# Attention's 64 by 64 products in groups of four, sums of weights on GpSimd, and a test ahead of an addition

## The chip, the core and the metric

The kernel runs on one core of a Trainium2 chip. The metric is the device time of one execution in microseconds (us), lower is better; times given are medians of several runs. A core has a matrix engine (TensorE, PE in the profile, with its weight loads as PEld), a vector engine (VectorE, DVE), a scalar engine (ScalarE, ACT), GpSimd (POOL) and a sync engine (SP) that here only issues transfers. Matrix products land in PSUM, which has eight banks of 2 KB per partition.

## The reference, cut to what matters

```python
# q, k, v: (8, 8, 576, 64); w_in 512 x 2048, w_out 2048 x 512
scores = scale * np.matmul(q_c, k_c.transpose(0, 1, 2, 4, 3))   # chunks of 64 positions
scores = scores - np.max(scores, axis=-1, keepdims=True)
attn = np.exp(scores)
attn = attn / (np.sum(attn, axis=-1, keepdims=True) + 1e-09)
out = np.matmul(attn, v_c)
x = out.transpose(0, 2, 1, 3).reshape(4608, 512)
h = x @ w1_in;  r = np.maximum(h, 0.0);  y = (s * (r * r) + b) @ w1_out
h = y @ w2_in;  g = h / (1.0 + np.exp(-1.702 * h));  result = g @ w2_out
```

Attention works inside chunks of 64 positions, and two feed-forward layers follow. Weights arrive as 64-bit floats.

## The kernel before, in words

The 4608 tokens are nine blocks of 512. A block of attention is four pairs of heads, and a pair has eight chunks, so 16 products of 64 by 64 for the scores (L287) and 16 for the second product with v (L271). Head h of the pair lies in partitions 64h to 64h + 63, for q, k, v and the result alike, so the products alternate between two quarters of the array: rows and columns 0 to 63, and rows and columns 64 to 127. Scores and second products each take one PSUM bank, out of two that rotate (tag "at"). Blocks 0 and 1 use `EarlyPair`, which loads and transposes otherwise and whose second product (L358) already runs over all four quarters into two banks. `split` and `split_x` turn a result into a high and a low part: ACT copies (L96), DVE subtracts (L97).

Each large product is three matmuls of 128 x 512 (low by high, high by high, high by low); `gemm_in` (L487) and `gemm_out` (L562) are the first layer, and the first block of the second. The other eight blocks of the second layer go in pairs through `Halves`, with seven products in place of eight (L658, L753); for that `sums` prepares sums and differences of quarters of the second weights. It loads four quarters into a staging buffer, GpSimd computes four sums (L193 to L196), ACT copies the rounded high part into a second staging buffer (L198), GpSimd subtracts it (L199), and SP stores both (L204). There are three staging buffers, and 32 calls of `sums`.

`decode` turns 64-bit weights into 32-bit ones: ACT scales the low words into c (L120), DVE shifts and merges the high words into t, which is m by its bits (L121, L124), GpSimd adds c to t (L128), ACT squares the high words into c (L129), DVE sets m to zero where that square is tiny (L131). In the opening `first_steps` spreads this over steps and then splits m (L146, L147); for the second weights `decode_second` issues it at once and GpSimd stores m (L177).

The order of the work is a list of items with due times in units, 32 units to a block; items of one time stand in order of their entry. A pair whose offset is o issues its scores at o + 1, its softmax from o + 2, the second product at o + 8 and the split at o + 8.5. Offsets are 7 units apart, in block 2 8 units. In the opening the steps follow `FIRST_STEPS`. A planner that simulates the engines makes each engine's queue out of this; each queue then runs strictly in its order.

Of the kernel before, what the change touches and what calls it, by code (L numbers as in the profile page):

```python
# [44 lines left out]
def chunk_attention_two_ffn(ctx, tc, q, k, v, w1_in, w1_out, s, b, w2_in, w2_out, out):  # L45
# [32 lines left out]
    h_ps = ctx.enter_context(tc.tile_pool(name="h_ps", bufs=2, space=PSUM))  # L78
    at_ps = ctx.enter_context(tc.tile_pool(name="at_ps", bufs=2, space=PSUM))
    dpool = ctx.enter_context(tc.tile_pool(name="dpool", bufs=1, space=DRAM))  # L80
# [9 lines left out]
    wi_sums = [dpool.tile([P, 7, 2, 2, P], F32, name=f"wi_sums{i}") for i in range(KF // 2)]  # L90
    wo_sums = dpool.tile([P, 7, KF // 2, 2, 2, P], F32, name="wo_sums")
    y_dram = [dpool.tile([P, KD, n], F32, name=f"y{j}") for j, n in enumerate(sizes)]

# [22 lines left out]
    def decode(st, m, c):  # L116

        high, low = st[:, :, 1], st[:, :, 0]
        t = m.bitcast(I32)
        nc.scalar.activation(out=c.bitcast(I32), in_=low.bitcast(U32), func=AF.Copy, scale=2.0 ** -29)  # L120
        nc.vector.tensor_scalar(  # L121
            out=t, in0=high, scalar1=3, scalar2=0x3FFFFFF8, op0=ALU.logical_shift_left, op1=ALU.bitwise_and
        )
        nc.vector.scalar_tensor_tensor(  # L124
            out=t, in0=high, scalar=-0x40000000, in1=t, op0=ALU.bitwise_and, op1=ALU.bitwise_or
        )
        yield
# [56 lines left out]
    def sums(kind, i, z):  # L184
# [18 lines left out]
        for part, src in enumerate((hi.bitcast(F32), q[:, 1:8, :])):  # L203
            nc.sync.dma_start(out=to[:, :, part, :], in_=src)  # L204


    def runs(j):

        c0, n = starts[j] // CH, sizes[j] // CH
        done = 0  # L210
        while done < n:
            bb, c = divmod(c0 + done, CPB)
            step = min(n - done, CPB - c)
            yield done, step, bb, c
            done += step

    heads = [slice(h * CH, (h + 1) * CH) for h in range(2)]

    class Pair:
# [20 lines left out]
        def load_v(self):  # L240
            self.v = apool.tile([P, self.nch, CH], F32, tag="vs", name="vs", bufs=HP)
            for off, m, bb, c in runs(self.j):
                for h in range(2):
                    rows = v[bb, 2 * self.hp + h, c * CH:(c + m) * CH, :]
                    nc.sync.dma_start(
                        out=self.v[h * CH:(h + 1) * CH, off:off + m, :], in_=rows.rearrange("(c p) d -> p c d", p=CH)
                    )

# [7 lines left out]
        def turn(self, p):  # L256
# [8 lines left out]
            return pt  # L265

        def second(self, pt):
            ps = at_ps.tile([P, self.n], F32, tag="at", name="xT")
            for c in range(self.nch):
                for r in heads:  # L270
                    nc.tensor.matmul(  # L271
                        out=ps[r, c * CH:(c + 1) * CH], lhsT=self.v[r, c, :], rhs=pt[r, c, :], start=True, stop=True
                    )
            return ps

        def split_x(self, ps):
            X[0, self.j, self.hp] = xh, xl = new_x()
            split(xh, xl, ps)

        def steps(self):  # L280

            yield from self.stage_qk()
            yield
            ps = at_ps.tile([P, self.nch, CH], F32, tag="at", name="sc")
            for c in range(self.nch):
                for r in heads:
                    nc.tensor.matmul(  # L287
                        out=ps[r, c, :], lhsT=self.qt[r, c * CH:(c + 1) * CH], rhs=self.kt[r, c * CH:(c + 1) * CH],
                        start=True, stop=True,
                    )  # L290
# [4 lines left out]
            nc.vector.tensor_reduce(out=mx, in_=ps, axis=AX.X, op=ALU.max)  # L295
            nc.vector.tensor_tensor(
                out=p, in0=ps, in1=mx.unsqueeze(2).to_broadcast([P, self.nch, CH]), op=ALU.subtract
            )
# [11 lines left out]
            yield  # L310
            ps = self.second(turned)
            yield
            self.split_x(ps)
            done[0, self.j] = done.get((0, self.j), 0) + 1

    class EarlyPair(Pair):
# [21 lines left out]
        def turn(self, p):  # L338
# [7 lines left out]
            return pt.rearrange("p (c h q) -> p c h q", h=2, q=CH)  # L346

        def second(self, pt):

            n = self.n // 2  # L350
            banks = (
                at_ps.tile([P, n], F32, tag="at", name="xT"),
                acc_ps.tile([P, n], F32, tag=f"acc{2 * (self.hp % 2) + 1}", name="xT"),
            )
            for c in range(self.nch // 2):
                for e, ps in enumerate(banks):
                    for h, r in enumerate(heads):
                        nc.tensor.matmul(  # L358
                            out=ps[r, c * CH:(c + 1) * CH],
                            lhsT=self.early.v[c][heads[e], (2 * self.hp + h) * D:(2 * self.hp + h + 1) * D],  # L360
                            rhs=pt[heads[e], c, h, :], start=True, stop=True,
                        )
            return banks

        def split_x(self, banks):
            X[0, self.j, self.hp] = x = new_x()
            xh, xl = (t.rearrange("p (c e t) -> p c e t", e=2, t=CH) for t in x)
            for e, ps in enumerate(banks):
                split(xh[:, :, e, :], xl[:, :, e, :], ps.rearrange("p (c t) -> p c t", t=CH))
            if self.j == 0:  # L370
                first_x.update((i.engine, i) for i in nc.cur_bb.bb.instructions[-2:])
            elif self.hp == HP - 1:
                marks.update((("x", i.engine), i) for i in nc.cur_bb.bb.instructions[-2:])

# [38 lines left out]
    def new_x():  # L413
        return tuple(xpool.tile([P, NB_MAX], F32R, tag=t, name=t) for t in ("xh", "xl"))
# [164 lines left out]

    HF, HK = KF // 2, KD // 2  # L580

    def minus(to, one, two):
        nc.vector.tensor_tensor(out=to, in0=one, in1=two, op=ALU.subtract)

    class Halves:
# [58 lines left out]
        def bank(self, key, bank, *tags):  # L644
            pool, tag = {"x": (acc_ps, tags[0]), "d": (at_ps, "at"), "b": (h_ps, "h")}[bank]
            self.ps[key] = pool.tile([P, NB_MAX], F32, tag=tag, name=bank)
# [270 lines left out]
```

## Time and profile before

| | |
|---|---|
| median of 3 runs | 1655.07 us (1652.5 to 1656.92) |
| the profiled execution | 1660.28 us |
| its span | 1658.5 us |
| TensorE busy | 1604.2 us, 97% |
| VectorE, ScalarE, GpSimd busy | 69%, 45%, 16% |
| mean granted TensorE clock | 0.99 |

The profile is of one execution. Busy time is a union of intervals; a matmul's own duration in a row overlaps its neighbours, so the distance between starts is the pace. In a timeline row "x32" are 32 records merged, and a bracket gives the idle time ahead and who ended it. A product of 64 by 64 in 32-bit floats stands as two records.

### The profile page before, as it was taken

To read this page: it belongs to the slowest core of one execution; us is meant where nothing else is said; L and a number is where in the kernel's file an instruction comes from. 1 tells how busy PE (TensorE), PEld (TensorE's weight loads), DVE (VectorE), ACT (ScalarE), POOL (GpSimd) and SP (SyncE) were. 2 spreads that over 40 slices of the span, in tenths; PEclk is the share of its full clock that TensorE was granted. 3 is DMA by queue.
4 is the path that set the end of the run, shared out by engine and by line. 5 is a ranking of instruction groups with operands and counts; after the bars stand their busy time and mean duration, and the time that the engine had idled before them with its cause. 6 is when DMAs were issued, how large, how long until landed. Compare 5 with 4: busy or idle time off the path is not lost.

```text
span 1658.5 us, 24595 instructions
## 1 busy us (share of the span) xinstructions
PE 1604.2 (97%) x8928; PEld 1312.8 (79%) x8928; DVE 1149.3 (69%) x1836; ACT 747.0 (45%) x1258; POOL 266.9 (16%) x294
## 2 busy tenths in 40 slices
PE   6879999999999999999999999999999999999998
PEld 5758887778788878888888888878887888788876
DVE  5876666867687775777757543579568946984685
ACT  3768543333333333333345532456345525653552
POOL 1322101333223223233333000000001000100000
PEclk9889999999999999999999999999999999999999
DMA  9435445656455554646456441676868686767654
GB/s 229 114 102 162 121 132 131 146 132 163 122 141 145 143 136 132 156 128 155 117 160 216 135 135 45 188 239 221 206 195 266 181 221 207 255 183 218 219 192 77
DMA packets 398345, 272.19 MB, mean 164 GB/s; under 512 B 255376, under 2 KB 345488, under 8 KB 398224
## 3 DMA queue, kind: packets, MB, share of 16 engines
q1 hardware_dynamic: 390800, 249.64, 55.0%
q0 software_dynamic: 5120, 16.78, 3.0%
q10 hardware_dynamic: 2304, 4.20, 0.7%
q8 instruction: 71, 1.16, 0.3%
q14 instruction: 50, 0.41, 0.1%
HBM read 209.72 MB, written 60.82 MB: 163 GB/s over the span
## 4 chain that ended last, share of the span: by engine, by line
PE 77%; DVE 8%; DMA 4%; SPq 3%; ACT 3%; issue 2%; POOL 2%; POOLq 0%; DVEq 0%; ACTq 0%
PE acc L562 19%; PE h L487 18%; PE x L658 11%; PE x L753 11%; PE d L658 5%; PE d L753 5%; PE b L658 3%; PE b L753 3%; SPq L235 2%; PE sc L287 1%; PE xT L271 1%; DVE gl L502 1%; DVE r L500 1%; DVE pt L261 1%; ACT gh L501 1%
## 5 line engine op out<-in xcount | busy, mean ns | idle before, releaser
L487 PE MATMUL h<-xh,wi 128*128 128x512 f32 x1280 | 402.7, 396 | 13.5 <-ACT r L517 5.4
L562 PE MATMUL acc<-gh,wo 128*128 128x512 f32 x1152 | 354.8, 394 | 6.0 <-ACT gh L96 3.7
L487 PEld LDWEIGHTS h<-xh,wi 128*128 128x128 f32 x1280 | 240.3, 190 | 66.3 <-ACT r L517 6.3
L562 PEld LDWEIGHTS acc<-gh,wo 128*128 128x128 f32 x1152 | 215.5, 189 | 53.0 <-ACT gh L96 4.1
L487 PE MATMUL h<-xl,wi 128*128 128x512 f32 x640 | 251.2, 394 | 0.0
L562 PE MATMUL acc<-gl,wo 128*128 128x512 f32 x576 | 220.3, 392 | 3.8 <-DVE gl L502 3.8
L501 ACT ACTIVATE gh<-r,sb 128x512 fp32r<-128x512 f32 x112 | 80.9, 723 | 184.4 <-DVE r L500 184.1
L500 DVE SCALAR_TENSOR_TENSOR r<-r,sb 128x512 f32<-128x512 f32 x112 | 103.9, 928 | 64.3 <-ACT r L499 63.8
L502 DVE SCALAR_TENSOR_TENSOR gl<-r,sb,gh 128x512 fp32r<-128x512 f32 x112 | 107.3, 959 | 57.2 <-ACT gh L501 57.1
L487 PEld LDWEIGHTS h<-xl,wi 128*128 128x128 f32 x640 | 121.7, 190 | 25.9
L562 PEld LDWEIGHTS acc<-gl,wo 128*128 128x128 f32 x576 | 108.1, 188 | 28.6 <-DVE gl L502 6.2
L128 POOL TENSOR_TENSOR wm<-wm,wc 128x512 int32<-128x512 int32 x52 | 75.7, 1459 | 338.6 <-DVE wm L124 176.9
L730 ACT ACTIVATE op<-wo 128x512 fp32r<-128x512 f32 x128 | 79.5, 630 | 79.4 <-PE d L753 25.9
L680 DVE TENSOR_TENSOR wo<-wo,r 128x512 f32<-128x512 f32 x96 | 66.0, 691 | 63.0 <-ACT r L679 62.6
L753 PE MATMUL x<-op,wi 128*128 128x512 f32 x432 | 104.4, 389 | 0.0
L658 PE MATMUL x<-xh,wi 128*128 128x512 f32 x320 | 99.5, 391 | 3.1 <-DVE wo L677 3.1
L261 DVE STREAM_TRANSPOSE pt<-p 32x256 f32<-32x256 f32 x224 | 97.7, 436 | 3.9
L597 POOL DMA_DIRECT2D xr<-y x32 | 17.3, 540 | 506.3 <-DVE op L731 262.8
L679 ACT ACTIVATE r<-wo 128x512 f32<-128x512 f32 x96 | 60.8, 633 | 76.8 <-DVE wo L677 76.0
L753 PEld LDWEIGHTS x<-op,wi 128*128 128x128 f32 x432 | 81.1, 188 | 16.9
L731 DVE TENSOR_TENSOR op<-wo,op 128x512 fp32r<-128x512 f32 x128 | 85.2, 680 | 7.4 <-ACT op L730 6.0
L198 ACT ACTIVATE wst<-wst 128x896 fp32r<-128x896 f32 x32 | 30.5, 953 | 128.1 <-POOL wst L196 83.5
(145 smaller groups left out, 2780.1 us busy)
## 6 DMA issues: line engine op xcount, KB each, us to landing
wi<-wo_sums SPq DMA_DIRECT2D x112, 512.0 KB, 3.9
wi<-wi_sums SPq DMA_DIRECT2D x96, 512.0 KB, 3.7
wst<-in_moe_w_out SPq DMA_DIRECT2D x32, 512.0 KB, 4.6
wi_sums<-wst SPq DMA_DIRECT2D x32, 448.0 KB, 3.6
wo_sums<-wst SPq DMA_DIRECT2D x32, 448.0 KB, 3.5
wst<-in_moe_w_in SPq DMA_DIRECT2D x24, 512.0 KB, 5.0
y<-ost SPq DMA_DIRECT2D x36, 256.0 KB, 3.3
xr<-y POOLq DMA_DIRECT2D x32, 256.0 KB, 6.1
```

The lines of the kernel that those rows point to most:

```text
L128: nc.gpsimd.tensor_tensor(out=t, in0=t, in1=c.bitcast(I32), op=ALU.add)
L261: nc.vector.transpose(out=pt[r.start + ek * BK:r.start + (ek + 1) * BK, :, eq * BK:(eq + 1) * BK], in_=p[r.start + eq * BK:r.start + (eq + ...
L487: nc.tensor.matmul(out=ps, lhsT=w_[:, kk, :], rhs=x_, start=kk == 0 and a == 0, stop=kk == KD - 1 and a == 2,)
L500: nc.vector.scalar_tensor_tensor(out=r, in0=r, scalar=s_ap, in1=r, op0=ALU.mult, op1=ALU.mult)
L501: nc.scalar.activation(out=gh, in_=r, func=AF.Identity, bias=b_ap)
L502: nc.vector.scalar_tensor_tensor(out=gl, in0=r, scalar=b_ap, in1=gh.bitcast(F32), op0=ALU.add, op1=ALU.subtract)
L562: nc.tensor.matmul(out=acc[m], lhsT=l_, rhs=r_, start=i == 0 and a == 0, stop=i == KF - 1 and a == 2)
L658: nc.tensor.matmul(out=self.ps[key], lhsT=l_, rhs=r_, start=start and k == 0 and a == 0, stop=k == HK - 1 and a == 2, skip_group_check=not ...
L680: nc.vector.tensor_tensor(out=g, in0=h, in1=r, op=ALU.mult)
L730: nc.scalar.activation(out=hi, in_=src, func=AF.Copy)
L731: nc.vector.tensor_tensor(out=lo, in0=src, in1=hi.bitcast(F32), op=ALU.subtract)
L753: nc.tensor.matmul(out=self.ps[key], lhsT=l_, rhs=r_, start=start and i == 0 and a == 0, stop=i == HF - 1 and a == 2, skip_group_check=not ...
```

## The change

Four things are edited. (1) One PSUM tile of two banks, `at_banks`, stays for the whole kernel; scores go into the left halves of both banks and second products into the right halves. Chunks of the first half of a block write bank 0 and run as before; chunks of the second half write bank 1 and cross over: the scores of head h land in the partitions of the other head, v is loaded into crossed partitions, and the second product crosses back. `quarters` issues chunk i for both heads and chunk i + 4 for both heads, so that four products in a row have four different quarters of the array. `load_v` cuts its loads at the half of the block. `EarlyPair` of block 0 takes banks of tag "h" and "acc" for its second product. `Halves` alternates by hand between the two banks. (2) In `sums` the copy of the high part and both stores move to GpSimd. (3) In `decode` the square goes to the low words of the staged weights, and the test comes ahead of GpSimd's addition.

```diff
-    at_ps = ctx.enter_context(tc.tile_pool(name="at_ps", bufs=2, space=PSUM))
+    at_ps = ctx.enter_context(tc.tile_pool(name="at_ps", bufs=1, space=PSUM))
+    at_banks = at_ps.tile([P, 2, NB_MAX], F32, name="at")
...
         yield
+        square = low.bitcast(F32)
+        nc.scalar.activation(out=square, in_=high.bitcast(F32), func=AF.Square)
+        nc.vector.scalar_tensor_tensor(out=m, in0=square, scalar=TINY * TINY, in1=m, op0=ALU.is_ge, op1=ALU.mult)
+        yield
         nc.gpsimd.tensor_tensor(out=t, in0=t, in1=c.bitcast(I32), op=ALU.add)
-        nc.scalar.activation(out=c, in_=high.bitcast(F32), func=AF.Square)
-        yield
-        nc.vector.scalar_tensor_tensor(out=m, in0=c, scalar=TINY * TINY, in1=m, op0=ALU.is_ge, op1=ALU.mult)
         yield
...
-        nc.scalar.activation(out=hi, in_=q[:, 1:8, :], func=AF.Copy)
+        nc.gpsimd.tensor_copy(out=hi, in_=q[:, 1:8, :])
...
-            nc.sync.dma_start(out=to[:, :, part, :], in_=src)
+            nc.gpsimd.dma_start(out=to[:, :, part, :], in_=src)
...
+    left, right = at_banks[:, :, 0:NB_MAX // 2], at_banks[:, :, NB_MAX // 2:NB_MAX]
+
+    def quarters(nch):
+        for i in range(nch // 2):
+            for e in range(2):
+                for h in range(2):
+                    yield e, i, e * (nch // 2) + i, h, heads[h], heads[h ^ e]
...
+                for e in range(2):
+                    a, z = max(off, e * half), min(off + m, (e + 1) * half)
+                    for h in range(2) if a < z else ():
+                        rows = v[bb, 2 * self.hp + h, (c + a - off) * CH:(c + z - off) * CH, :]
+                        nc.sync.dma_start(
+                            out=self.v[heads[h ^ e], a:z, :], in_=rows.rearrange("(c p) d -> p c d", p=CH)
+                        )
...
         def second(self, pt):
+            for e, i, c, h, r, other in quarters(self.nch):
+                nc.tensor.matmul(
+                    out=right[r, e, i * CH:(i + 1) * CH], lhsT=self.v[other, c, :], rhs=pt[other, c, :],
+                    start=True, stop=True,
+                )
...
+            ps = self.room_scores().rearrange("p e (c t) -> p e c t", t=CH)
+            for e, i, c, h, r, other in quarters(self.nch):
+                nc.tensor.matmul(
+                    out=ps[other, e, i, :], lhsT=self.qt[r, c * CH:(c + 1) * CH], rhs=self.kt[r, c * CH:(c + 1) * CH],
+                    start=True, stop=True,
+                )
...
+        def room_scores(self):
+            return right if self.j == 0 and self.hp % 2 else left
...
+            if self.j == 0:
+                self.ps = (
+                    h_ps.tile([P, n], F32, tag="h", name="xT"),
+                    acc_ps.tile([P, n], F32, tag=f"acc{2 * (self.hp % 2) + 1}", name="xT"),
+                )
+            else:
+                self.ps = right[:, 0, :], right[:, 1, :]
...
         def bank(self, key, bank, *tags):
+            if bank == "d":
+                self.ps[key] = at_banks[:, next(turns) % 2, :]
+                return
```

## Rows read from the trace of the kernel before

**Rows 1.** The page, busy us with share of the span, and instructions.
```profile
PE 1604.2 (97%) x8928; PEld 1312.8 (79%) x8928; DVE 1149.3 (69%) x1836; ACT 747.0 (45%) x1258; POOL 266.9 (16%) x294
```

**Rows 2.** The chain that ended last, share of the span by engine.
```profile
PE 77%; DVE 8%; DMA 4%; SPq 3%; ACT 3%; issue 2%; POOL 2%; POOLq 0%; DVEq 0%; ACTq 0%
```

**Rows 3.** Stretches: length, busy PE, PEld, DVE, ACT, POOL, granted clock, DMA, GB/s.
```profile
46.00:125.00 79.00, 64.88 (x495) 51.38 (x494) 62.63 (x103) 55.23 (x103) 24.39 (x18) 0.89 0.33 103
...
235.00:310.00 75.00, 70.62 (x478) 55.72 (x474) 52.42 (x90) 29.39 (x48) 13.01 (x14) 1.00 0.56 136
310.00:440.00 130.00, 125.64 (x815) 102.74 (x814) 94.93 (x155) 43.80 (x70) 37.56 (x42) 0.99 0.58 143
440.00:570.00 130.00, 130.00 (x842) 107.01 (x841) 97.77 (x155) 47.24 (x76) 39.80 (x45) 1.00 0.53 133
```

**Rows 4.** Timeline of PE at two places: start, length, instructions merged.
```profile
83.26 0.69 PE L358 MATMUL xT<-pt,wo 64*64 64x64 f32 x32
83.78 1.11 PE L287 MATMUL sc<-kt,qt 64*64 64x64 f32 x32
...
400.25 1.15 PE L271 MATMUL xT<-pt,vs 64*64 64x64 f32 x32
401.24 1.10 PE L287 MATMUL sc<-kt,qt 64*64 64x64 f32 x32
```

**Rows 5.** Timeline of PE, windows 400.25 to 400.27 and 93.93 to 93.96.
```profile
400.25 0.27 PE L271 MATMUL xT<-pt,vs 64*64 64x64 f32 x2
...
93.93 0.29 PE L358 MATMUL xT<-pt,wo 64*64 64x64 f32 x4 [1.93 <-DVE pt L345]
```

**Rows 6.** Waits: who waited for whom, us in total, times, longest.
```profile
ACT wst L198 <- POOL wst L196: 83.5, 18, 9.9
...
ACT wc L129 <- POOL wm L128: 30.7, 39, 2.9
```

**Rows 7.** Timeline where PE stops; in brackets idle time before, and who ended it.
```profile
274.12 0.73 PE L487 MATMUL h<-xh,wi 128*128 128x512 f32 x2 [1.17 <-ACT r L499]
...
337.52 0.95 ACT L198 ACTIVATE wst<-wst 128x896 fp32r<-128x896 f32 x1 [9.94 <-POOL wst L196]
...
339.00 0.73 PE L487 MATMUL h<-xh,wi 128*128 128x512 f32 x2 [2.23 <-ACT r L499]
...
591.33 0.75 DVE L500 SCALAR_TENSOR_TENSOR r<-r,sb 128x512 f32<-128x512 f32 x1
...
592.39 2.10 POOL L199 TENSOR_TENSOR wst<-wst 128x896 fp32r<-128x896 f32 x1 [1.96 <-ACT wst L198]
...
592.95 2.09 DVE L502 SCALAR_TENSOR_TENSOR gl<-r,sb,gh 128x512 fp32r<-128x512 f32 x1 [0.87 <-ACT gh L501]
...
595.10 0.50 PE L562 MATMUL acc<-gl,wo 128*128 128x512 f32 x1 [1.39 <-DVE gl L502]
```

**Rows 8.** Groups by line and shape: busy us, mean ns, idle us before, releaser.
```profile
L287 PE MATMUL sc<-kt,qt 64*64 64x64 f32 x1152 | 45.7, 232 | 0.5 <-ACT kt L336 0.5
...
L271 PE MATMUL xT<-pt,vs 64*64 64x64 f32 x896 | 33.8, 221 | 0.0
...
L96 ACT ACTIVATE xh<-xT 128x512 fp32r<-128x512 f32 x28 | 16.4, 585 | 7.9 <-PE xT L271 7.9
...
L97 DVE TENSOR_TENSOR xl<-xT,xh 128x512 fp32r<-128x512 f32 x28 | 19.2, 684 | 21.1 <-ACT xh L96 21.1
...
L199 POOL TENSOR_TENSOR wst<-wst 128x896 fp32r<-128x896 f32 x32 | 68.1, 2129 | 50.0 <-ACT wst L198 50.0
...
L177 POOL DMA_DIRECT2D w_wi<-wm x16 | 9.1, 570 | 31.7 <-DVE wm L131 31.7
```

**Rows 9.** The chain that ended last, opening: start, length, what.
```profile
10.53 1.99 PE sc L287 x32
...
25.05 1.29 POOL wi L128
...
26.36 0.70 ACT wi L129
```

More of the change, by code (lines that the diff above doesn't have):

```diff
@@ L1 @@
+from itertools import count
 import concourse.bass as bass
@@ L241, in load_v @@
             self.v = apool.tile([P, self.nch, CH], F32, tag="vs", name="vs", bufs=HP)
+            half = self.nch // 2
             for off, m, bb, c in runs(self.j):
[L243 to L247, printed above, removed]
+                for e in range(2):
[5 more added lines that the diff above has]
+                        )
         def stage_qk(self):
@@ L265, in turn, with split_x @@
             return pt
+        def room_scores(self):
+            return left
         def second(self, pt):
[L268 to L278, printed above, removed]
+            for e, i, c, h, r, other in quarters(self.nch):
[3 more added lines that the diff above has]
+                )
+        def split_x(self):
+            X[0, self.j, self.hp] = x = new_x()
+            split(*(t.rearrange("p (e n) -> p e n", e=2) for t in x), right)
         def steps(self):
@@ L283, in steps @@
             yield
[L284 to L290, printed above, removed]
+            ps = self.room_scores().rearrange("p e (c t) -> p e c t", t=CH)
[4 more added lines that the diff above has]
+                )
             yield
@@ L294, in steps @@
             p = tmp("p")[:, 0:self.n].rearrange("p (c t) -> p c t", t=CH)
-            nc.vector.tensor_reduce(out=mx, in_=ps, axis=AX.X, op=ALU.max)
+            by_bank = mx.rearrange("p (e c) -> p e c", e=2)
+            nc.vector.tensor_reduce(out=by_bank, in_=ps, axis=AX.X, op=ALU.max)
             nc.vector.tensor_tensor(
-                out=p, in0=ps, in1=mx.unsqueeze(2).to_broadcast([P, self.nch, CH]), op=ALU.subtract
+                out=p.rearrange("p (e c) t -> p e c t", e=2), in0=ps,
+                in1=by_bank.unsqueeze(3).to_broadcast([P, 2, self.nch // 2, CH]), op=ALU.subtract,
             )
@@ L310, in steps @@
             yield
-            ps = self.second(turned)
+            self.second(turned)
             yield
-            self.split_x(ps)
+            self.split_x()
             done[0, self.j] = done.get((0, self.j), 0) + 1
@@ L346, in turn, with room_scores @@
             return pt.rearrange("p (c h q) -> p c h q", h=2, q=CH)
+        def room_scores(self):
+            return right if self.j == 0 and self.hp % 2 else left
         def second(self, pt):
             n = self.n // 2
[L351 to L354, printed above, removed]
+            if self.j == 0:
[5 more added lines that the diff above has]
+                self.ps = right[:, 0, :], right[:, 1, :]
             for c in range(self.nch // 2):
-                for e, ps in enumerate(banks):
+                for e, ps in enumerate(self.ps):
                     for h, r in enumerate(heads):
+                        of = h ^ (c >= self.nch // 4)
                         nc.tensor.matmul(
@@ L360, in second, with split_x @@
                             lhsT=self.early.v[c][heads[e], (2 * self.hp + h) * D:(2 * self.hp + h + 1) * D],
-                            rhs=pt[heads[e], c, h, :], start=True, stop=True,
+                            rhs=pt[heads[e], c, of, :], start=True, stop=True,
                         )
-            return banks
-        def split_x(self, banks):
+        def split_x(self):
             X[0, self.j, self.hp] = x = new_x()
[L367 to L373, printed above, removed]
+            xh, xl = (t.rearrange("p (c e t) -> p e c t", e=2, t=CH) for t in x)
+            if self.j:
+                split(xh, xl, right.rearrange("p e (c t) -> p e c t", t=CH))
+                if self.hp == HP - 1:
+                    marks.update((("x", i.engine), i) for i in nc.cur_bb.bb.instructions[-2:])
+                return
+            for e, ps in enumerate(self.ps):
+                split(xh[:, e], xl[:, e], ps.rearrange("p (c t) -> p c t", t=CH))
+            first_x.update((i.engine, i) for i in nc.cur_bb.bb.instructions[-2:])
     class Early:
@@ L580, in chunk_attention_two_ffn @@
     HF, HK = KF // 2, KD // 2
+    turns = count()
     def minus(to, one, two):
@@ L644, in bank @@
         def bank(self, key, bank, *tags):
-            pool, tag = {"x": (acc_ps, tags[0]), "d": (at_ps, "at"), "b": (h_ps, "h")}[bank]
+            if bank == "d":
+                self.ps[key] = at_banks[:, next(turns) % 2, :]
+                return
+            pool, tag = {"x": (acc_ps, tags[0]), "b": (h_ps, "h")}[bank]
             self.ps[key] = pool.tile([P, NB_MAX], F32, tag=tag, name=bank)
```

## The prediction

> **What bounds the kernel now.** I read the page's busy times first: TensorE is busy for 1604.2 of 1658.5 us [rows 1], so this is a TensorE kernel, and only a shorter TensorE queue or less TensorE idling can pay. The chain that ended last says the same: 77% of it is PE [rows 2]. Then the table of busy time by stretch [rows 3], because a mean of 97% can hide a slow opening. It does: between 46 and 125 us PE is busy 64.88 of 79 us at a granted clock of 0.89. In the attention blocks after it PE has no idle time from 440 to 570 us, and lacks 4.4 us of 75 and 4.4 us of 130 in the two stretches shown before that. VectorE fills 97.77 of 130 us there, three quarters, ScalarE and GpSimd about a third each. So in the blocks every microsecond of PE work that vanishes is a microsecond of span, as long as the other engines keep up. Then I read the PE timeline around the small products [rows 4, 5], and last the waits of ACT and the timeline where PE stops [rows 6, 7], for what the other two parts of the edit can reach.
>
> **Part one, four products at a time.** A pair's scores are 16 products of 64 by 64 that go out as alternating (rows 0, columns 0) and (rows 64, columns 64), and so are its second products. Each is recorded as two matmuls, so 32 records make one set. The set of L271 starts at 400.25 and its successor at 401.24: 0.99 us [rows 4]. The opening's EarlyPair already uses all four quarters of the array in its second product, and there the set of 32 starts at 83.26 and its successor at 83.78: 0.52 us [rows 4]. The starts show why: in the first 20 to 30 ns two records of L271 start, and four of L358 [rows 5]. The new order of the quarters is (0,0), (64,64), (0,64), (64,0), four different ones in a row, so I take the L358 pace for it: 0.99 - 0.52 = 0.47 us per set. L271 has 896 records and L287 1152 [rows 8], which is 28 sets and 36 sets. Of L287's sets 8 belong to the opening, so blocks 2 to 8 have 28 + 28 = 56 sets: 56 x 0.47 = **26.3 us off PE**. Bounds: nothing (still two abreast) and 56 x 0.52 = 29 us (no row has so much).
>
> One thing differs from L358: there each row half writes a bank of its own, here both banks take products of both row halves. L271 already sends both row halves into one bank, and they start together [rows 5], so I see no reason for a slower pace. The Trainium skill's page "PSUM — Partial Sum Buffer" (section "PSUM bank collisions raise a hardware error") says that different row tiles can't access one bank at the same time, and its own measurements limit this to the same quadrant of partitions too; in the new order two products that share a bank write different partition halves. Read strictly, the rule would leave two abreast and part one would be worth nothing; the two simultaneous starts in one bank speak for the narrow reading.
>
> The eight score sets of the opening shorten as well. The first is on the chain, 1.99 us for 32 records at a low clock [rows 9], of which I take half, and one set of block 1 stands on PE right behind another (83.78) and gives 0.47. Together **1.4 us**; at least 0, at most 8 sets x 0.9 = 7.
>
> Scores and second products now live in two halves of the same two banks for the whole kernel, where before they rotated through separate ones. If a bank is kept to one engine at a time, a score set waits until the split of the pair before has read the bank: ACT L96 0.585 and DVE L97 0.684 [rows 8], 1.27 us. Behind it on PE stand the gemm sets, and everything that feeds on them. In blocks 3 to 8 the plan issues second product and next scores at the same unit, ahead of the split, and the timeline has them side by side (400.25, 401.24); there it is the split that waits, some 0.5 us, and its x is wanted many units later. In blocks 1 and 2 the split stands half a unit or more ahead of the next scores, six places: 6 x 1.27 = 7.6 us if PE stands still each time, 0 if the planner puts gemm sets between. I take **+1**.
>
> **Part two, sums wholly on GpSimd.** ACT loses L198, and above all its waiting: 83.5 us behind POOL's subtractions, the longest 9.9 [rows 6]. What that does to PE can be seen at 337.52: L198 (0.95 us) has waited 9.94, the relu L499 stands behind it, and PE stops 2.23 us for that relu [rows 7]. Another such stop, of 1.39, ends at 595.10 [rows 7]; two more lie at 297 and 425 us. PE's missing time in rows 3 and this stop are 4.4 + 4.4 + 1.4 = 10.2 us; of it three stops between 268 and 278 us, 2.8 together, the longest at 274.12 [rows 7], lie under an unbroken DVE queue and not under L198. So 7.4 us could go. POOL takes the copy over. Its price is not in the trace: not under ACT's 0.95, and not above POOL's two-input operation of the same shape, L199, 2.13 us [rows 8]; I take 1.6. SP loses 64 stores and the waits ahead of them, and gains 48 loads of v: each run is cut at the half of its block, two pieces more per pair, except in block 4, where a batch ends there anyway. POOL gains 64 issues; L177 costs 0.57 us for 128 runs of 2 KB [rows 8], a sum's store has 896 runs of 512 bytes, so 0.57 to 7 x 0.57 = 4.0 us each; I take 1.5, nearer to the row of the same engine. POOL then has 32 x 1.6 + 64 x 1.5 = 147 us more over the 520 us from 310 to 834, in which it is idle two thirds of the time: it fits.
>
> What it costs is DVE. While POOL ran L199 for 2.10 us at 592.39, DVE's L502 took 2.09 us; L500, of the same kind and shape, took 0.75 just before, at 591.33 [rows 7]. A two-input DVE operation stands still as long as POOL works on two inputs. The copy may do this for another 32 x 1.6 = 51 us, in a time in which DVE is free for a quarter of 520, 130 us: hidden in the mean, not at each place. The Trainium skill's "GPSIMD Engine Reference" (section Key points) names this contention for VectorE instructions with two SBUF inputs; the row agrees, and whether a one-input copy on GpSimd does it no run here shows. I therefore count **6 us** of the 7.4 as won, with 12 and -4 as the ends.
>
> **Part three, the test moved ahead.** Square goes to the unused low words and no longer overwrites the operand of POOL's addition, so ACT's wait there (30.7 us in 39 places, [rows 6]) ends. In the opening the chain ran POOL 1.29, then ACT's Square 0.70 [rows 9], then DVE's test and the split; now Square runs beside DVE's first operations and the test ahead of POOL, so only the 0.70 leaves the chain. Between 25 and 100 us the chain makes this turn about five times: 5 x 0.7 = **3.5 us**; at least 0 (other order edges set the pace), at most 8. The new wait is POOL's on DVE's test; behind it on POOL stand other additions and, later, the sums and their stores, and who waits for those is the next load of a staging buffer on SP, ahead of its use.
>
> **Sum.** -26.3 - 1.4 + 1 - 6 - 3.5 = -36.2 us. Span 1658.5 - 36.2 = 1622.3; the profiled execution took 1660.28, 1.8 outside the span, so 1624.1; that execution is 5.2 above the median 1655.07, which gives **1619** for a median. I say 1620.
>
> **Rivals.** (a) *DVE eats part of it.* POOL's copies, stores and subtractions hold DVE at bad moments, and PE, 4% faster, has less slack: the 6 us don't come and a third to a half of part one is lost: 1655 - 26.3/2 - 4 = 1638, to 1647. For it: the 2.09 us row. Against: DVE at 75%. Chance 0.16. (b) *Still two abreast*, part one worth nothing: 1655 - 6 - 3.5 = 1646, to 1651 where the others come small. Chance 0.06. (c) *PE waits for the bank*: the planner puts the split ahead of the next scores in all blocks, so that PE stands 1.27 us or more in 28 places: 28 x 1.27 = 36 us against 36 won, no change; with 0.5 us of queueing more on ACT and DVE it is 50 us and 1668. It decides from 36 / 28 = 1.3 us per place. For it: both halves share both banks. Against: the side-by-side order of [rows 4]. Chance 0.06, half of it slower. (d) *POOL becomes the bound*, slower too: in 130 us POOL is busy 39.80 [rows 3] and does a quarter of the 32 sums, 8 copies and 16 stores. With copies at 2.1 its free 90 us are full when a store takes (90 - 17) / 16 = 4.6 us; then staging buffers come free late, and SP, which issues in order, holds the q, k and v loads behind them. At 5.5 us it is 15 us over in each of four such stretches: 1655 - 36 + 60 = 1679. Against: the 0.57. Chance 0.04.
>
> **How the numbers follow.** My forecast has 0.68: its own range is 1604 to 1636. With (a) and part of (b) the range 1603 to 1647 holds 8 in 10. A measurement of this kernel can tell about 0.3% (5 us) from no change. Faster: 0.68 + 0.16 + 0.04 of (b) = 0.88; the rest of (b) and half of (c) 0.05 the same; half of (c) and (d) 0.07 slower.
>
> **What would show it.** Right: sets of 32 small records take 0.5 us start to start, four starting together; ACT has no wait for POOL in the sums; PE idles under 4 us from 160 us to the end of the attention. Wrong: small sets near 1 us; PE idle ahead of the scores with ACT xh or DVE xl as releaser; DVE's two-input operations longer and PE idle behind gl; POOL's stores of several us each and SP waiting for staging buffers.

## The result and the profile after

The changed kernel takes 1673.27 us (median of 4, 1671.44 to 1676.38) beside 1655.99 us for the kernel before: ratio 1.0105 [1.0091, 1.0120], 17 us slower. The forecast was 1620, in a range of 1603 to 1647: wrong by its sign and outside its range.

The page's busy line for TensorE, the twin of [rows 1], says in one number that the work did shrink: 11.3 us less of PE in a span that is 11.1 us longer (1669.6 for 1658.5). The small products alone lost more, 31.3 us by the groups below (26.8 + 21.4, for 45.7 + 33.8 in [rows 8]); the other matmuls took 20 us longer, at a mean granted clock of 0.977 (0.990 before), and PE's idle time grew by 22.4 (76.7 for 54.3).

```profile
PE 1592.9 (95%) x8928; PEld 1293.2 (77%) x8928; DVE 1183.2 (71%) x1832; ACT 720.6 (43%) x1222; POOL 364.9 (22%) x390
```

The timeline of PE shows why the work shrank. This is one pair of sets of the changed kernel, to be held against 400.25 and 401.24 in [rows 4]; then the groups of lines (busy, mean ns, idle before, releaser).

```profile
403.42 0.69 PE L292 MATMUL at<-pt,vs 64*64 64x64 f32 x32
403.93 0.65 PE L307 MATMUL at<-kt,qt 64*64 64x64 f32 x32
```

```profile
L204 POOL TENSOR_TENSOR wst<-wst 128x896 fp32r<-128x896 f32 x32 | 74.3, 2322 | 1.4
...
L203 POOL CAST wst<-wst 128x896 fp32r<-128x896 f32 x32 | 34.9, 1092 | 58.8 <-DMA wi_sums<-wst 31.5 <-DMA wo_sums<-wst 26.2
...
L209 POOL DMA_DIRECT2D wo_sums<-wst x32 | 29.2, 913 | 41.9 <-issue 37.8 <-DVE mx L316 4.1
...
L209 POOL DMA_DIRECT2D wi_sums<-wst x32 | 29.0, 906 | 48.7 <-issue 48.7
...
L307 PE MATMUL at<-kt,qt 64*64 64x64 f32 x1152 | 26.8, 232 | 2.7 <-DVE p L317 2.2 <-ACT kt L358 0.5
...
L292 PE MATMUL at<-pt,vs 64*64 64x64 f32 x896 | 21.4, 225 | 0.0
```

A set of 32 records now gives way to the next after 0.51 us, where it was 0.99. In the blocks of attention, however, PE now stands idle more than before. These are the stretches of [rows 3] (length, then busy PE, PEld, DVE, ACT, POOL, granted clock, DMA share, GB/s):

```profile
46.00:125.00 79.00, 63.95 (x497) 49.46 (x496) 63.46 (x99) 50.17 (x91) 24.63 (x17) 0.89 0.30 101
...
235.00:310.00 75.00, 71.69 (x525) 56.26 (x524) 53.68 (x91) 29.71 (x48) 14.41 (x16) 0.98 0.52 132
310.00:440.00 130.00, 123.87 (x820) 100.15 (x819) 101.62 (x156) 40.90 (x67) 60.11 (x62) 0.97 0.55 144
440.00:570.00 130.00, 120.85 (x787) 95.90 (x786) 88.73 (x135) 38.33 (x63) 57.79 (x62) 0.95 0.50 134
...
700.00:830.00 130.00, 122.93 (x869) 98.60 (x868) 103.82 (x163) 42.87 (x70) 55.96 (x61) 0.96 0.45 127
```

From 440 to 570 us PE lacks 9.2 us and from 700 to 830 us 7.1, where it lacked none, and the granted clock of these two stretches is 0.95 and 0.96, where it was 1.00. GpSimd is busy 60 of 130 us at most; its waits for its own transfers are not in this figure.

In places on the time axis: the first score set of block 2 starts at 164.3 us (161.0 before), the last small set of attention at 848.7 (833.4), and what follows takes 820.9 (825.1). So the opening lost 3.3 us, attention's blocks lost 12.0, and the rest won 4.2. Attention by itself, between these places, in the kernel before and in the changed one (the same columns):

```profile
161.01:833.39 672.38, 662.10 (x4365) 540.43 (x4364) 490.42 (x800) 260.24 (x417) 183.34 (x201) 1.00 0.54 138
```

```profile
164.33:848.66 684.33, 655.23 (x4365) 525.54 (x4364) 512.92 (x799) 235.68 (x386) 263.31 (x281) 0.97 0.50 134
```

In it the small products shrank by some 25 us (64.6 to 39.8 by their groups). But PE's idle time grew by 18.8 us, and the large matmuls took some 18 us longer, at a granted clock of 0.97 where it was 1.00. So a stop of PE is paid for twice here: as idle time, and in slower matmuls.

The waits say who held PE up. First the table over the whole execution (who waited for whom, us in total, times, longest; "issue" is waiting for nothing that the profile shows), then that of SP's queue of transfers, SPq:

```profile
POOL wi_sums L209 <- issue: 48.7, 16, 5.0
...
ACT wc L124 <- DMA wst<-in_moe_w_in: 43.0, 9, 9.2
...
POOL wo_sums L209 <- issue: 37.8, 15, 3.3
...
DVE wm L125 <- DMA wst<-in_moe_w_in: 36.8, 8, 7.6
...
ACT wc L124 <- DMA wst<-in_moe_w_out: 35.3, 7, 9.5
...
DVE wm L125 <- DMA wst<-in_moe_w_out: 25.7, 6, 6.1
```

```profile
SPq L118 <- DMA wi_sums<-wst: 55.2, 10, 12.9
...
SPq L112 <- DMA wo_sums<-wst: 53.1, 10, 12.1
```

ACT's wait for GpSimd's subtraction (83.5 us in [rows 6]) is gone as forecast. In its place ACT and DVE wait 141 us for the loads of second weights (43.0 + 36.8 + 35.3 + 25.7), and SP waits 108 us to start these loads, because the staging buffer that they go to is still being stored. GpSimd waits 86.5 us ahead of the stores of sums (48.7 + 37.8), and another 40.2 ahead of its stores of decoded weights (L182), which before waited for DVE alone (L177 in [rows 8]). One such turn, from the timelines of POOL, SP, ACT, DVE and PE of the changed kernel:

```profile
677.08 2.12 POOL L204 TENSOR_TENSOR wst<-wst 128x896 fp32r<-128x896 f32 x1
679.13 0.92 POOL L209 DMA_DIRECT2D wo_sums<-wst  x1
...
683.86 0.92 POOL L209 DMA_DIRECT2D wo_sums<-wst  x1 [3.31 <-issue]
...
689.30 1.28 POOL L203 CAST wst<-wst 128x896 fp32r<-128x896 f32 x1 [4.04 <-DMA wo_sums<-wst]
690.66 2.40 POOL L204 TENSOR_TENSOR wst<-wst 128x896 fp32r<-128x896 f32 x1
...
683.61 0.39 SPq L112 DMA_DIRECT2D wst<-in_moe_w_in  x1
...
687.96 0.68 ACT L124 ACTIVATE wc<-wst 128x512 int32<-128x512 uint32 x1 [8.83 <-DMA wst<-in_moe_w_in]
...
687.98 0.43 DVE L125 TENSOR_SCALAR wm<-wst 128x512 int32<-128x512 int32 x1 [7.64 <-DMA wst<-in_moe_w_in]
...
691.05 2.56 DVE L534 SCALAR_TENSOR_TENSOR gl<-r,sb,gh 128x512 fp32r<-128x512 f32 x1
...
693.67 0.80 PE L594 MATMUL acc<-gl,wo 128*128 128x512 f32 x1 [2.33 <-DVE gl L534]
694.26 1.05 PE L594 MATMUL acc<-gh,wo 128*128 128x512 f32 x2
...
696.75 0.62 PE L594 MATMUL acc<-gh,wo 128*128 128x512 f32 x2
```

The store of the high parts goes out at 679.13 and lands some 4.2 us later; only then, at 683.61, can SP start the load into that buffer. SP stood still from 676.15. The load lands at 687.96, and until then ACT has stood 8.83 us and DVE 7.64, with the activations of the first weights' products queued behind them. When DVE goes on, L534, for which PE waits, is the fifth operation in its queue, and it takes 2.56 us beside GpSimd's subtraction of 690.66; PE stops 2.33 us for it. From 693.7 to 696.5, behind the stop, the granted clock is 0.50, the lower of its two levels (1.2 GHz), and two matmuls take 1.05 us; from 696.8 to 700 it is 1.00 (2.4 GHz), and two take 0.62.

### The profile page after: what moved, and what is told of

Same layout as the page of the kernel before. It is cut to its first block, busy times and chain, and to the rows that moved or that the text cites. A ratio compares the mean times of both kernels' runs of the same rounds, so it can differ in the third digit from the quotient of the medians.

```text
span 1669.6 us, 24650 instructions
## 1 busy us (share of the span) xinstructions
PE 1592.9 (95%) x8928; PEld 1293.2 (77%) x8928; DVE 1183.2 (71%) x1832; ACT 720.6 (43%) x1222; POOL 364.9 (22%) x390
## 4 chain that ended last, share of the span: by engine, by line
PE 51%; DVE 1%; ACT 0%; issue 0%; ACTq 0%
PE x L789 10%; PE x L694 10%; PE acc L594 7%; PE h L519 7%; PE at L694 5%; PE at L789 5%; PE b L694 3%; PE b L789 3%; DVE wo L716 0%; DVE pt L281 0%; ACT r L715 0%; PE at L292 0%; PE at L307 0%; DVE p L327 0%; DVE gl L534 0%
## 5 line engine op out<-in xcount | busy, mean ns | idle before, releaser
L594 PE MATMUL acc<-gh,wo 128*128 128x512 f32 x1152 | 363.0, 403 | 15.3 <-ACT gh L533 8.8
L594 PEld LDWEIGHTS acc<-gh,wo 128*128 128x128 f32 x1152 | 220.8, 194 | 65.1 <-ACT gh L533 10.6
L594 PE MATMUL acc<-gl,wo 128*128 128x512 f32 x576 | 225.4, 402 | 12.3 <-DVE gl L534 12.2
L534 DVE SCALAR_TENSOR_TENSOR gl<-r,sb,gh 128x512 fp32r<-128x512 f32 x112 | 113.2, 1012 | 50.7 <-ACT gh L533 50.7
L532 DVE SCALAR_TENSOR_TENSOR r<-r,sb 128x512 f32<-128x512 f32 x112 | 109.0, 976 | 21.8 <-ACT r L531 21.3
L531 ACT ACTIVATE r<-h 128x512 f32<-128x512 f32 x112 | 65.8, 587 | 77.7 <-PE h L519 69.4
```

The costliest lines, as they stand in the source:

```text
L532: nc.vector.scalar_tensor_tensor(out=r, in0=r, scalar=s_ap, in1=r, op0=ALU.mult, op1=ALU.mult)
L534: nc.vector.scalar_tensor_tensor(out=gl, in0=r, scalar=b_ap, in1=gh.bitcast(F32), op0=ALU.add, op1=ALU.subtract)
L594: nc.tensor.matmul(out=acc[m], lhsT=l_, rhs=r_, start=i == 0 and a == 0, stop=i == KF - 1 and a == 2)
```

## The experiments

Three theories were set against each other at first. **A**: the stores on GpSimd go out late, staging buffers come free late, and so do SP's loads. **B**: GpSimd's copy is what hurts, since it holds DVE up. **C**: parts one and three are to blame. Each kernel is given by its edit of the changed kernel (or of the kernel before, where said); ratios are to the kernel before, run beside it (medians of 1654.86 to 1656.96 us).

**Part two in pieces.** stores_sp puts the stores back on SP, copy_act the copy back on ACT, sums_old both; part2 is the kernel before with part two alone.

```
stores_sp  -  nc.gpsimd.dma_start(out=to[:, :, part, :], in_=src)
           +  nc.sync.dma_start(out=to[:, :, part, :], in_=src)
copy_act   -  nc.gpsimd.tensor_copy(out=hi, in_=q[:, 1:8, :])
           +  nc.scalar.activation(out=hi, in_=q[:, 1:8, :], func=AF.Copy)
sums_old   both;   part2: the reverse of both, in the kernel before
```

> The changed kernel with the 64 stores of the sums issued by SP again; the copy stays on GpSimd. Theory A (GpSimd issues the stores late and waits between the two of a pair, so staging buffers come free late, SP's load of the next weights waits for their landing, and ACT and DVE wait in order for that load): the 108 us of SP waiting on the landing of sums fall under 30, ACT's and DVE's waits on the weight loads (141 us) fall under 30, and the time is 1625 to 1640. Theory B (GpSimd's copy holds DVE at their common memory port): the copy is still there, time 1660 to 1675. Theory C (the test moved ahead, or the four at a time, keeps buffers longer): 1660 to 1675.

> The changed kernel with the copy of the sums on ACT again; the stores stay on GpSimd. Theory A: the stores are still late, and ACT's wait for GpSimd's subtractions comes back, 1665 to 1685. Theory B: 1630 to 1645, and DVE's two-input operations get shorter by the 35 us of copies at most. Theory C: 1660 to 1675.

> Copy on ACT and stores on SP again: the four at a time and the test moved ahead alone. Theories A and B: the loss was in the sums, 1625 to 1640. Theory C: still 1655 or more.

> The kernel before with the sums wholly on GpSimd and nothing else. Theory A: SP waits for landings of the sums as in the changed kernel, some 100 us in 20 places, and the time is 1675 to 1700. Theory B: slower as well, 1665 to 1690, with SP not waiting. Theory C: 1650 to 1660.

Measured: stores_sp **1637.19** (0.9880 [0.9865, 0.9895]), copy_act **1698.15** (1.0244 [1.0225, 1.0263]), sums_old **1662.03** (1.0027 [1.0016, 1.0038]), part2 **1683.81** (1.0171 [1.0149, 1.0193]). Stores on GpSimd cost 36 us, with either place of the copy (1673 - 1637, 1698 - 1662), as A has it. Its chain of waits came true in part: in stores_sp SP's waits for landings fall from 108 to 7 us, but those of ACT and DVE for loads only from 141 to 76, where A expected under 30. In copy_act, which came out above A's range, loads are hardly waited for (10 us); there it is ACT's own copy that waits, 171 us (134 in sums_old). B falls: taking the copy away from GpSimd makes the kernel 25 us slower. But the copy does hold DVE, as stores_sp's timelines show. In the first two rows an operation that takes 0.75 us alone takes 1.45 beside the copy. In the last two it began 0.06 us ahead of the copy and took its 0.75, and the copy took 1.48 for 0.93; so the one that begins second waits:

```profile
294.77 0.93 POOL L203 CAST wst<-wst 128x896 fp32r<-128x896 f32 x1
...
294.79 1.45 DVE L532 SCALAR_TENSOR_TENSOR r<-r,sb 128x512 f32<-128x512 f32 x1
...
491.50 0.75 DVE L532 SCALAR_TENSOR_TENSOR r<-r,sb 128x512 f32<-128x512 f32 x1 [0.91 <-ACT r L531]
491.56 1.48 POOL L203 CAST wst<-wst 128x896 fp32r<-128x896 f32 x1
```

sums_old, at which A and B expected 1625 to 1640, leaves something for C: parts one and three alone bring nothing.

**One part at a time.** part1 has the products alone, part3 (an edit of the kernel before) decoding alone; p1_copy is the products with the copy on GpSimd, copy_pool the kernel before with that copy. C1 and C3 split theory C: the banks or the opening (C1), or decoding's order (C3).

```
part1      sums_old, and decode() as in the kernel before
part3      the kernel before, and decode() as in the changed kernel
p1_copy    stores_sp, and decode() as in the kernel before
copy_pool  the kernel before, and  nc.gpsimd.tensor_copy(out=hi, in_=q[:, 1:8, :])
```

> Only the four-at-a-time products (with the two fixed banks, the new loads of the values and the opening's changed banks); sums of second weights and decoding are those of the kernel before. Theory A (only the stores on GpSimd hurt; parts one and three are worth what was forecast): 1656 - 26 = 1630 us, between 1625 and 1636. Theory C1 (the new bank order or the opening gives the products' gain back, decoding's new order costs nothing): about 1662, as the kernel with parts one and three did. Theory C3 (decoding's new order is what gave it back): 1630 here too, and part three alone is slower than before by some 30 us.

> Only decoding's new order (test for tiny numbers ahead of GpSimd's addition); products and sums are those of the kernel before. Forecast's own term: 1656 - 3.5 = 1652 us. Theory C3 (the decoding now ends on GpSimd, so the split of the weights waits for GpSimd's queue): 1675 to 1690 us, with waits of ACT and DVE on GpSimd's addition. Theory C1: 1650 to 1660.

> Four-at-a-time products, the sums' copy on GpSimd, stores on SP, decoding as in the kernel before. The same with the new decoding was 1637. Theory C3 (the new decoding costs time): under 1632, down to 1620. If decoding's order is worth nothing: 1634 to 1640. The forecast's term: 1641.

> The kernel before with the sums' copy moved from ACT to GpSimd alone, stores on SP. Theory: with products two at a time PE is the bound in attention and ACT's waits for GpSimd's subtraction are hidden there, so 1650 to 1656 (gain of 0 to 6). Rival: the copy is worth 25 us with the old products too, as it is with the new (1637 against 1662): 1631. If the copy's gain shows only with the new products, the products' gain had been held by ACT's waits on GpSimd.

Measured: part1 **1663.99** (1.0044 [1.0027, 1.0061]), part3 **1656.74** (1.0000 [0.9989, 1.0012]), p1_copy **1638.94** (0.9896 [0.9881, 0.9911]), copy_pool **1650.41** (0.9962 [0.9949, 0.9975]). Decoding's order is worth nothing in the whole time, so C3 falls. The products alone cost 7 us, as C1 expected, but with the copy on GpSimd they win 11.5 (1650.4 to 1638.9). p1_copy has the same banks and the same opening as part1, so these are not what cost the products their gain. The two edits need each other: the copy is worth 6 us with the old products and 25 with the new. part1's timelines show the reason at one place, ACT first and then PE:

```profile
341.31 0.95 ACT L202 ACTIVATE wst<-wst 128x896 fp32r<-128x896 f32 x1 [6.81 <-DMA wo_sums<-wst]
342.17 0.70 ACT L532 ACTIVATE gh<-r,sb 128x512 fp32r<-128x512 f32 x1
...
342.92 1.22 PE L593 MATMUL acc<-gh,wo 128*128 128x512 f32 x2 [5.36 <-ACT gh L532]
```

ACT's copy waits 6.81 us, the activation behind it is late, and PE, which comes to its next products sooner than before, stands 5.36 us. In all of part1's attention PE stands 13.9 us for gh, where the kernel before had 2.1. The same queue on ACT was in the kernel before; that the slower products covered most of it there [rows 7] is argued from these waits, not tested by itself.

**Which resource the stores take.** A spare staging buffer (with one working tile less, for room) and half of the stores. Working tiles are the ten temporary tiles of 128 x 512 (`tpool`) that decoding, the activations and `Halves` share. In theory **A2** it is GpSimd's own time that the stores take, and not the buffers.

```
after_t9   -  tc.tile_pool(name="tpool", bufs=10)       +  bufs=9
after_st4  the same, and tc.tile_pool(name="stpool", bufs=3)   ->  bufs=4
half_sp    +  (nc.gpsimd, nc.sync)[part].dma_start(out=to[:, :, part, :], in_=src)
sp_st4     stores_sp with the edits of after_st4
```

> The changed kernel with 9 working tiles in place of 10, to be the base for a fourth staging buffer, which needs the room. All theories: no change or a little slower, 1673 to 1680.

> The changed kernel, stores on GpSimd, with four staging buffers in place of three (and 9 working tiles). Theory A in full (the stores hurt only through staging buffers that come free late, so that the loads of second weights on SP's queue land late): a spare buffer gives most of the 36 us back, 1637 to 1650, and the waits of ACT and DVE for those loads fall from 141 us to under 60. Rival A2 (GpSimd's own time is the bound: its stores and waits add to each set of sums and to the additions in decoding): 1665 to 1675, as the queue is as long as before.

> The changed kernel with the store of the high parts on GpSimd and that of the low parts on SP: one store of two on GpSimd. If the loss goes by the number of stores on GpSimd: halfway, 1655. If it is the last store's lateness that counts (the wait behind the subtraction): near 1637 to 1642.

> Stores on SP, copy on GpSimd, and four staging buffers (9 working tiles). With three it was 1637. If SP's loads still wait for staging buffers there (the trace has 48 us of such waits, behind decoding's test), a fourth takes some 5 to 12 us more: 1625 to 1632. If what is left of the forecast's gain is lost elsewhere: 1635 to 1640.

Measured: after_t9 **1693.18** (1.0217 [1.0194, 1.0240]), after_st4 **1661.18** (1.0030 [1.0019, 1.0041]), half_sp **1652.82** (0.9976 [0.9966, 0.9986]), sp_st4 **1647.46** (0.9947 [0.9929, 0.9965]). The expectation for the base missed: a working tile less costs 20 us. The traces place it: what follows the last small set of attention takes 839.0, 841.0 and 840.1 us in after_t9, after_st4 and sp_st4, and 820.9 in the changed kernel. Against that base the fourth buffer gives 32 us, with every store still on GpSimd. In after_st4's waits GpSimd waits for its stores of sums as long as before (87 us), and ACT and DVE hardly at all:

```profile
POOL wo_sums L209 <- issue: 45.2, 14, 4.7
...
POOL wi_sums L209 <- issue: 41.8, 15, 4.0
...
ACT wc L124 <- DMA wst<-in_moe_w_in: 6.0, 4, 1.9
...
ACT wc L124 <- DMA wst<-in_moe_w_out: 2.9, 2, 2.1
...
DVE wm L125 <- DMA wst<-in_moe_w_in: 2.2, 2, 1.8
...
DVE wm L125 <- DMA wst<-in_moe_w_out: 1.9, 1, 1.9
```

So most of the cost comes through the buffers (A). after_st4's time lies between the ranges of A (to 1650) and A2 (from 1665), with the missing tile in it. And with four buffers the stores on GpSimd still cost 14 us (1661.2 beside sp_st4's 1647.5), where it was 36 with three. SP still waits 98 us for landings in after_st4, and 19 in sp_st4; whether the 14 us are these waits or GpSimd's own time (A2) stays open. half_sp gives back 20 of 36 us, about by the number of stores. The waits of ACT and DVE for loads do not measure the loss one to one: in half_sp they are still 118 us. sp_st4 missed too: it is 10 us slower than stores_sp. That is the missing tile: at the last small set of attention sp_st4 is 4.3 us ahead (808.3 for 812.7), and behind it it loses 19.

**Where the products' gain went.** open_old undoes the changed banks of the opening; dec_late gives the loads of second weights more time; the light pair leaves out most of the second weights' work: decoding is one copy of the high words, and sums are stored unsplit.

```
open_old   stores_sp, and
           -  return right if self.j == 0 and self.hp % 2 else left
           +  return left
           -  h_ps.tile([P, n], F32, tag="h", name="xT"),
           +  right[:, 0, :],
dec_late   stores_sp, and decode_second's second step at t + 3.0 for t + 2.0
light_old  the kernel before, light_new the kernel part1, both without decode() for
           second weights and without the sums' copy and subtraction
```

> Stores on SP, copy on GpSimd, products four at a time (1637), and in the opening the score sets all in the one fixed pair of banks and the first block's second products in the other, in place of a bank of the first weights' products. Theory: the first weights' products start near 30 us as before, and 3 to 5 us come back: 1632 to 1634. Rival (the opening's time is set by decoding, not by banks): 1636 to 1639.

> Stores on SP, copy on GpSimd, products four at a time (1637), and each decoding of second weights planned one unit (about 3 us) later behind its load. Theory (ACT and DVE wait in order for these loads, 76 us in all, and hold up the activations of the first weights' products): waits fall by half or more and 2 to 8 us come back, 1629 to 1635. Rival (the buffer then comes free later, so the next load is as late): 1635 to 1642.

> The kernel before with most of the second weights' work left out: decoding is one copy of the high words, and the sums are stored unsplit (no copy, no subtraction), same loads and stores. All theories: PE alone sets attention, so as fast as the kernel before less its stops: 1638 to 1652.

> The same work left out, products four at a time, decoding of the first weights as before. Theory (the products' gain is eaten by the second weights' work on DVE, ACT and GpSimd): 20 to 27 us under light_old. Rival (the new banks, or the loads of values in halves, cost it): about 10 us under light_old.

Measured: open_old **1633.19** (0.9863 [0.9846, 0.9879]), dec_late **1638.02** (0.9895 [0.9881, 0.9910]), light_old **1648.19** (0.9958 [0.9943, 0.9973]), light_new **1629.54** (0.9844 [0.9829, 0.9859]). By the ratios open_old wins 3 us on stores_sp, though the intervals overlap. What it repairs is in PE's timeline. The changed kernel's opening:

```profile
24.88 0.68 PE L389 MATMUL xT<-pt,vs 64*64 64x64 f32 x16
29.18 1.12 PE L389 MATMUL xT<-pt,vs 64*64 64x64 f32 x16 [3.62 <-ACT kt L358]
...
41.91 0.79 PE L519 MATMUL h<-xh,wi 128*128 128x512 f32 x1
```

and open_old's:

```profile
24.56 0.68 PE L350 MATMUL qkT<-ident,wo 128*128 128x128 f32 x4
28.35 1.22 PE L519 MATMUL h<-xh,wi 128*128 128x512 f32 x2 [3.11 <-DVE wi L152]
```

Block 0's second products take a bank of the first weights' products, whose first matmul therefore comes at 41.91 in place of 28.35 (29.03 in the kernel before), and PE's stops there stay empty. With open_old block 2's scores start at 161.3, as before the change. Its two edits were not set apart. dec_late fell to its rival: the buffer is held longer, so the next load is late again (68 us of waits for 76). The light pair: without the second weights' work, and so with one staging buffer to a set of sums, the products are worth 18.7 us, a little under the 20 to 27 expected, with 2 us of the opening still lost.

**A way to need fewer buffers.** Both are edits of open_old.

```
open_hi_first  the store of the high parts ahead of GpSimd's subtraction
open_hi2       for first, n in ((1, 4), (5, 3)):
                   src = q[:, first:first + n, :]
                   hi = stpool.tile([P, 4, P], F32R, tag="hi", name="hi", bufs=1)[:, 0:n, :]
                   copy, subtraction and two stores on SP, for these n sums
```

> As the kernel with the opening's banks as before (1633), but the store of the high parts stands ahead of GpSimd's subtraction, some 2.2 us sooner. Theory (late staging buffers are what is left): 1 to 4 us faster, 1629 to 1632. Rival (SP's queue reaches the loads no sooner): 1632 to 1635.

> As the same kernel, but the high parts have one buffer of 128x512 of their own, used for four sums and then for three, so that a set of sums holds one staging buffer and not two; the copy of the last three sums waits for the first store to land, some 3 us of GpSimd. Theory: the waits of ACT and DVE for the loads fall below 30 us in all (76 with three buffers and two per set) and the kernel takes 1622 to 1630. Rival (GpSimd's wait for the landing holds up its additions for decoding, which is as bad): 1633 to 1645.

Measured: open_hi_first **1632.17** (0.9852 [0.9838, 0.9867]), not to be told from open_old; open_hi2 **1628.84** (0.9829 [0.9812, 0.9845]), the fastest of all: 28 us under the kernel before and 44 under the changed one. Its waits for second weights' loads are next to nothing, and PE is without idle time in the two stretches where the changed kernel lacked 6 and 9 us:

```profile
DVE wm L125 <- DMA wst<-in_moe_w_out: 1.5, 1, 1.5
...
ACT wc L124 <- DMA wst<-in_moe_w_out: 1.0, 1, 1.0
```

```profile
310.00:440.00 130.00, 130.00 (x892) 106.38 (x892) 104.11 (x160) 44.88 (x73) 56.83 (x68) 1.00 0.63 160
440.00:570.00 130.00, 130.00 (x893) 106.38 (x892) 102.94 (x168) 45.03 (x74) 54.32 (x69) 1.00 0.56 145
```

## Why the prediction was wrong

**Part two is the step that failed**, sum and sign: -6 was forecast, and the kernel with part two alone is 28 us slower than the one before (1683.8). The late release of staging buffers was put at nothing. Its two halves are opposite. The copy on GpSimd is worth 6 us with the old products and 25 with the new; the stores on GpSimd cost 33 us (part2 against copy_pool) to 36. The price of a store was not the error: 0.91 us were measured where 1.5 was taken. With 1.35 us of waiting on average (86.5 us in 64 stores) it is 2.3, and 2.9 with the 40 us that the stores of decoded weights now wait, still below the 4.6 that rival (d) asked for. The error was the test itself: "it fits" compared GpSimd's work with its free time, and a staging buffer is not freed by free time but by the landing of a store, which now stands behind a 2.3 us subtraction and behind the store before it. The sentence (under part three) that SP's next load is "ahead of its use" rested on no row, and it was the whole question: with three buffers the loads had no such lead. A fourth buffer takes the cost from 36 to 14 us; what those 14 are is open. So the mechanism named in rival (d), with a chance of 0.04, came true without its condition, and the loads that were waited for are those of second weights, where (d) had q, k and v.

**The clock was not priced.** The forecast took each stop of PE at its length. In attention the idle time grew by 18.8 us and the large matmuls, at the lower mean clock, by 18: together they ate the 25 us of the small products and 12 more.

**A rule read too late.** The Trainium skill's page "DMA: Bandwidth & Descriptors" (section "SWDGE vs HWDGE vs iDMA") gives plain transfers to SP or ACT and to GpSimd only what accumulates, casts or is irregular. These stores are plain, and the runs agree with it by 33 to 36 us; the prediction looked at the stores' price and not at this rule.

**Part one was right as a mechanism**, and too large as a term. A set takes 0.51 us in place of 0.99, so 56 sets give some 27 us off PE; the doubt about a shared bank is settled for this order of products, in favour of the narrow reading that the prediction took. Of this, 11.5 us reach the end with the copy on GpSimd, 18.7 with most of the second weights' work left out, and -7 alone. Rival (a) had said that PE would have less slack and lose a third to a half: right in kind, but the first to run out of slack was ACT, behind its own copy, which the forecast counted as a gain of part two only.

**The opening** was to win 1.4 us, and part three's 3.5 besides, and lost 3.3. Its first score set did shorten, to 1.14 us from 1.99. The forecast priced the two shared banks (1 us) and overlooked that block 0's second products move to a bank of the first weights' products; open_old, which gives it back, shows about the size.

**Part three** was to bring 3.5 us and brings none (part3, 1.0000); under 2 us between p1_copy and stores_sp can't be told from nothing. What leaves the chain as Square comes back in part as a wait behind GpSimd's addition, which now ends decoding: ahead of block 2 ACT's split waits 15 us for it in part3, where ACT's Square waited 9. In the one trace of part3 block 2's scores do start at 157.1 us, 3.9 sooner than before, so the opening may have gained what was forecast; the medians show none of it, and where it is lost again stays open.

**Banks.** Rival (c) was wrong: no 36 us of PE waiting for scores' banks; in attention PE's waits end on gl (12.2 us) and gh (11.3), and ahead of the scores on nothing. Not forecast at all was the win after attention, 4.2 us: one wait of 0.8 us in each of the four last passes (3.1 us in the trace of before) is gone in the changed kernel, and in part1 too; the new order of the banks is a likely cause, which no run set apart.

The terms as the runs give them, in the order copy, products, decoding, stores: -6 - 11.5 - 2 + 36 = +16.5, beside 17 measured. As each run differs from the next by one edit, from the kernel before to the changed one, they have to add up; the sum is a list and not a test, and in another order the terms differ.

## What to carry to other kernels

Before moving transfers to another engine, read how long the buffer that they empty stays taken, and what the next load into it has as a lead over its first reader; the mean load of the engine answers neither. When the bounding engine is made faster, look for in-order queues whose waits it used to cover: here one edit was worth 6 us before and 25 after another. Price a stop of the bounding engine above its length, where its clock falls behind the stop. A small buffer that leaves a set of sums one large buffer in place of two (open_hi2) gave more than an earlier store (open_hi_first) or a later use (dec_late).

## What the hardware showed that was not expected

- A store of 896 runs of 512 bytes takes GpSimd 0.91 us to issue, and the next store from GpSimd began only about when the one before had landed: 679.13 and 683.86, with 4.2 us from issue to landing by the page of the profile. With one store of the two on GpSimd (half_sp) there is no such wait. Why it waits stays open (the kernel sets dynamic_dma_scratch_size=1024; a larger one was not tried).
- GpSimd's copy with one input (0.93 us for 128x896) holds a two-input operation of VectorE as its two-input operations do: 1.45 us for 0.75. The prediction's sentence that VectorE stands still as long as GpSimd works holds only where GpSimd began first; where VectorE began first, the copy took 1.48 us for 0.93. The move paid nevertheless.
- Four 64 by 64 products of which two and two share a bank run as fast as those with a bank to each row half: 0.51 and 0.52 us a set.
- One working tile of ten taken away cost 20 us, more than any of the three parts was to bring but the first, and 18 us of it after attention.
